# A fused attention and MLP kernel on one core: ScalarE's own SiLU from chunk 1 on, chunk 0 in two token parts, Strassen's scheme in all four groups of chunks 3 to 8, and a new order

## The chip, the cores and the metric

The kernel runs on one core of a Trainium2 chip. The metric is the time of one execution on the device, in microseconds. The runs of the kernel before spread from 271.2 to 278.7 us over the chips of this study, most of them near 273.5 or near 276, so every kernel was timed beside the kernel before on the same chip. A run more than 1.5% above the fastest of its kernel counts as slow and is left out of the ratios. Stages are compared in the profiles, where single instructions have times. Each profile is one execution. All stage times count from the start of the profiled span. The engines are named PE (TensorE, matmuls), DVE (VectorE), ACT (ScalarE), POOL (GpSimd) and SP (SyncE, which here only starts DMAs).

## The reference, cut to what matters

```python
q_s = softmax(q, axis=-1)            # q, k, v: (8, 8, 576, 64) float32
k_s = softmax(k, axis=2)             # over the 576 positions
kv  = einsum('bhsd,bhse->bhde', k_s, v)
x   = einsum('bhsd,bhde->bhse', q_s, kv)   # then (4608, 512)
h   = x @ w_in                       # 512 -> 2048
g   = h * sigmoid(h)                 # SiLU
out = g @ w_out                      # 2048 -> 512, float32
```

## The kernel before

Tokens go through the two layers in nine chunks: chunk 0 has 576 tokens, chunk 1 has 448, the others 512. While chunk t is multiplied, the attention of batch t+1 is prepared. For a batch that means: load q, k and v by DMA; exponentials on ACT (`eq`, `ek`); the sums over q's rows on DVE (`zq`, `rzq`); the normalization of q on POOL (`eq<-eq,rzq`); one transposing DMA of all of q (`qT<-eq`); a cast of v (`vaug`); the kv products on PE, their normalization (`kvn`); and at last the product `o<-qT,kvn`, whose cast is `XT`, the input of the next chunk's first layer. Chunk 2 needs batch 2, so all of this has to be done for batch 2 by the end of chunk 1.

The first layer of chunks 3 to 8 is done in four groups of features, three of them by Strassen's scheme (seven products instead of eight, on sums of weights `TX` and sums of inputs `XS`), the second layer of chunks 1 to 8 wholly by it (sums of weights `TW`, sums of activations `SW`). The sums are made by DVE or POOL. Chunks 0 and 1 compute SiLU by way of tanh (ACT) and a product (DVE), the later chunks by ACT's own SiLU:

```python
STD = 2
def act1(t, fb):
    for off, size in part[t]:
        hps = HP.pop((t, fb, off))
        if t < STD:
            sg = mp.tile([128, TCH], FP32, name="sg", bufs=2)
            nc.scalar.activation(out=sg[:, 0:size], in_=hps[:, 0:size], func=ACT.Tanh, scale=0.5)
        ...
            if t < STD:
                nc.vector.scalar_tensor_tensor(out=y, in0=sg[:, h], scalar=1.0,
                    in1=hps[:, h], op0=ALU.add, op1=ALU.mult)
            else:
                nc.scalar.activation(out=y, in_=hps[:, h], func=ACT.Silu)
```

Each engine is given its instructions in a fixed order, and a table says at which position of a chunk each operation is put. One entry, for chunk 1 (`ex`: exponentials of q and k, `qs`: sums, `qn`: normalization, `vs`: casts of v, `tp`: transposing DMA, all of batch 2):

```python
1: {'ex': [0.9, 4.4, 5.9, 5.4], 'qs': [3.9, 4.9], 'qn': [4.91, 5.91], 'vs': [9.3, 10.9],
    ..., 'tp': 11.4, ...},
...
put(b - 1, p["qs"][cc], qsum, b, cc)
put(b - 1, p["qn"][cc], qnorm, b, cc, G)       # G is GpSimd
```

The prologue handles all of batch 0's q at once and keeps PE busy with dummy matmuls (`heat`) between its steps:

```python
heat(24)
for cc in range(2):
    exp(0, "qt", "eq", cc); qsum(0, cc); qnorm(0, cc, nc.vector)
exp(0, "kt", "ek", 0); vcast(0, 0, nc.scalar)
exp(0, "kt", "ek", 1); vcast(0, 1, nc.scalar)
tr(0, 0); trcopy(0, 0)
heat(5)
kv(0, 0); kvcopy(0, 0)
heat(1)
...
```

The softmax here doesn't subtract the row's maximum and nothing guards it: scores larger than these inputs give would overflow.

Of the kernel before, what the change touches and what calls it, by code (L numbers as in the profile page):

```python
# [15 lines left out]
PLAN = {  # L16
    0: {'y': [5.5, 6.5, 7.5, 8.5, 8.5, 9.5, 10.5, 11.5, 13.5, 13.8, 14.5, 15.5, 15.6, 15.7, 15.9, 22.5], 'ex': [8.9, 10.9, 12.9, 13.4], 'qs': [9.92, 11.4], 'qn': [10.43, 11.41], 'vs': [14.45, 15.05], 'ks': [15.65, 15.75], 'kc': [15.651, 15.751], 'lq': 14.06, 'tp': 12.9, 'ox': [16.35, 16.6], 'oc': [16.36, 18.61], 've': [2, 2]},
    1: {'ex': [0.9, 4.4, 5.9, 5.4], 'qs': [3.9, 4.9], 'qn': [4.91, 5.91], 'vs': [9.3, 10.9], 'ks': [12.4, 13.9], 'kc': [13.41, 14.91], 'lq': 10.45, 'lk': 12.4, 'lv': 15.41, 'tp': 11.4, 'ox': [16.4, 23.6], 'oc': [17.91, 23.61], 've': [1, 1], 'pa': [13.1, 17.7, 18.3], 'pae': [1, 0, 0]},
    2: {'std': 2, 'order': [(3, 1), (2, 1), (2, 6), (3, 6), (2, 2), (2, 7), (3, 2), (3, 7), (3, 5), (2, 5), (2, 4), (3, 3), (3, 4), (2, 3)], 'y': [-2.5, 1.5, 3.5, 4.5, 5.5, 7.5, 9.5, 11.5, 14.0, 15.5, 17.5, 19.0, 20.0, 21.0], 'ex': [-2.6, 0.41, 2.92, 0.43], 'qs': [2.9, 3.9], 'qn': [5.91, 5.91], 'vs': [3.42, 12.4], 'ks': [8.9, 16.4], 'kc': [10.91, 16.41], 'lq': -0.55, 'lk': -2.1, 'lv': 14.41, 'tp': 7.4, 'ox': [18.4, 19.4], 'oc': [18.91, 19.41], 'sl': [0.5, 1.5, 3, 3, 4.5, 8.5, 7, 7], 'add': {(3, 2): 17.02, (2, 7): 13.55, (3, 1): 10.02, (3, 6): 11.55, (2, 5): 17.55, (2, 3): 21.55, (3, 3): 19.55}, 'act': {(2, 6): 13.02, (2, 4): 19.02, (2, 3): 25.02, (2, 5): 17.55, (3, 2): 14.55, (3, 3): 23.02, (2, 1): 11.55, (3, 1): 9.55, (2, 7): 16.02}, 's1': {2: 0, 3: 0}, 'xs': [0.4, 0.9, 7.9, 4.4], 'pa': [16.45, 23.95, 19.45], 'ya': {3: 22.45, 6: 5.5, 5: 15.95, 2: 7.95}, 'm1': [1, 0], 'pb': [-0.4, 0.2, 2.1, 2.2, 2.8], 'xe': [0, 1, 1, 1], 'pae': [1, 1, 1], 'pbe': [0, 0, 0, 0, 0], 've': [1, 2]},
}  # L20
STEADY = {'std': 1, 'order': [(1, 1), (1, 6), (1, 2), (1, 7), (1, 5), (2, 1), (2, 6), (1, 4), (1, 3), (2, 2), (2, 7), (2, 5), (3, 1), (2, 4), (3, 6), (2, 3), (3, 7), (3, 2), (3, 5), (3, 4), (3, 3)], 'y': [1.5, 3.5, 5.5, 7.5, 9.5, 10.0, 15.5, 16.5, 17.5, 18.0, 22.0, 23.5, 24.2, 24.6], 'ex': [-5.1, -0.59, -4.08, -4.57], 'qs': [5.4, 6.4], 'qn': [5.91, 6.41], 'vs': [0.4, 7.42], 'ks': [11.9, 17.4], 'kc': [15.91, 17.41], 'lq': 9.95, 'lk': 16.9, 'lv': 9.41, 'tp': 8.9, 'ox': [22.4, 22.4], 'oc': [22.91, 23.41], 'sl': [2.0, 2.0, 6.5, 4.0], 'add': {(2, 2): 17.02, (1, 2): 6.55, (3, 2): 20.55, (3, 1): 16.55, (3, 7): 21.02, (1, 5): 9.55, (3, 5): 22.55}, 'act': {(1, 5): 12.02, (2, 6): 12.02, (1, 2): 7.02, (3, 1): 19.02, (1, 6): 9.02, (1, 1): 8.02, (3, 3): 25.55, (3, 5): 25.02, (1, 3): 14.02, (2, 2): 15.02, (2, 5): 16.55, (1, 4): 13.02, (3, 7): 23.02, (3, 6): 20.02}, 's1': {1: 1, 2: 0, 3: 0}, 'xs': [-1.6, 0.9, -1.6, 1.4], 'pa': [21.45, 21.95, 23.45], 'pb': [-0.05, 2.46, 2.95, -0.04, 2.95], 'ya': {4: 23.95, 5: 19.45}, 'm1': [0, 0], 'xe': [0, 0, 0, 0], 'pae': [1, 0, 0], 'pbe': [0, 0, 0, 0, 1], 've': [1, 1]}
for _t in range(3, 8):
    PLAN[_t] = STEADY
PLAN[8] = {'std': 1, 'order': [(1, 1), (1, 6), (1, 7), (1, 2), (1, 5), (2, 1), (2, 6), (1, 4), (1, 3), (2, 7), (3, 1), (2, 5), (2, 2), (3, 6), (2, 4), (2, 3), (3, 7), (3, 2), (3, 5), (3, 4), (3, 3)], 'y': [4.5, 5.0, 5.0, 7.5, 9.5, 10.5, 15.5, 17.5, 18.0, 19.0, 22.0, 23.7, 25.5, 26.6], 'sl': [4.0, 10.0, 7.5, 6.0], 'add': {(1, 2): 9.02, (3, 1): 16.02, (1, 5): 9.55}, 'act': {(2, 5): 18.02, (1, 3): 13.02, (1, 4): 15.02, (1, 6): 8.02, (2, 3): 22.02, (3, 3): 25.55, (3, 2): 24.02, (2, 1): 11.02, (3, 5): 22.55, (1, 5): 9.55, (3, 1): 15.55, (1, 2): 8.02, (1, 1): 5.02, (1, 7): 10.02, (2, 4): 19.02, (2, 2): 20.02, (2, 7): 16.02}, 's1': {1: 1, 2: 1, 3: 0}, 'xs': [-11.1, -0.1, 3.4, 7.9], 'pa': [19.95, 20.95, 22.95], 'pb': [-5.55, -4.04, 4.45, -0.04, 2.95], 'ya': {6: 9.5, 3: 27.05, 2: 10.95, 5: 20.95, 1: 7.0, 7: 18.95, 4: 25.7}, 'm1': [0, 0], 'xe': [0, 0, 0, 0], 'pae': [0, 0, 0], 'pbe': [0, 0, 0, 1, 0]}
PLAN[9] = {'y': [0, 1, 2, 3, 4, 5, 6, 7, 8, 9, 10, 11, 12, 13], 'ya': {}, 'm1': [0, 0], 'pb': [-0.5, -0.4, -0.3, 1.9, 2.9], 'pbe': [0, 0, 0, 0, 0]}
TXAT = [(0, (0, 11.76, 1, 0)), (1, (0, 15.77, 1, 0)), (2, (0, 14.78, 1, 1)), (3, (0, 15.79, 1, 1)), (0, (2, 3.1, 0, 0)), (1, (2, 5.6, 0, 0)), (2, (2, 5.6, 0, 0)), (3, (2, 9.6, 0, 1))]
TWAT = [(0, 10.1, 1), (0, 8.7, 1), (0, 13.0, 1), (0, 13.6, 1), (0, 14.7, 0), (0, 19.3, 1), (0, 17.9, 1), (0, 14.0, 1)]

@with_exitstack
def kernel(  # L30
# [26 lines left out]
    part = [[(0, 5 * P), (5 * P, S - 5 * P)]] + [[(0, cut[t + 1] - cut[t])] for t in range(1, NCH)]  # L57
# [34 lines left out]
    def load(b, name, src, ccs=None, eng=nc.sync):  # L92
        if name not in st[b]:
            st[b][name] = ld.tile([128, NG, J * D], FP32, name=name, bufs=LDB[name])
        x = src[b].rearrange("(g r) (p j) d -> g (r p) (j d)", r=2, j=J).rearrange("g x y -> x g y")
        c = slice(0, NG) if ccs is None else slice(2 * ccs, 2 * ccs + 2)
        eng.dma_start(out=st[b][name][:, c, :], in_=x[:, c, :])
# [4 lines left out]
    def exp(b, src, dst, cc):  # L102
        if dst not in st[b]:
            st[b][dst] = ap.tile([128, J, NG * D], BF16, name=dst, bufs=1)
        o = st[b][dst][:, :, cc * 128:(cc + 1) * 128].rearrange("p j (g d) -> p j g d", d=D)
        nc.scalar.activation(out=o, in_=jgd(st[b][src], cc), func=ACT.Exp)  # L106

    def vcast(b, cc, eng):
        o = vaug.rearrange("p j (g e) -> p j g e", e=E1)[:, :, 2 * cc:2 * cc + 2, 0:D]
        if eng is nc.scalar:  # L110
            eng.copy(out=o, in_=jgd(st[b]["vt"], cc))
        else:
            eng.tensor_copy(o, jgd(st[b]["vt"], cc))

    def qsum(b, cc):
# [3 lines left out]
        e = st[b]["eq"][:, :, cc * 128:(cc + 1) * 128].rearrange("p j (g d) -> p j g d", d=D)  # L119
        nc.vector.reduce_sum(out=st[b]["zq"][:, cc], in_=e, axis=AX.X)  # L120
# [15 lines left out]
    def tr_dma(b, eng):  # L136
# [3 lines left out]
        )  # L140

    TG = 6

    def tr(b, g):
        t = ps.tile([128, TG, 128], BF16, name="qtps", tag="ring", bufs=PSB["ring"])
        st[b]["qtps", g] = t
# [541 lines left out]
```

## Time and profile before

The time before the prediction was a median of 272.63 us (272.16 to 273.13, three runs). The profiled execution has a span of 270.6 us. By stages:

| stage | kernel before | length |
|---|---|---|
| first first-layer matmul | 16.65 us | 16.65 |
| chunk 1 starts | 48.90 | 32.25 |
| chunk 2's first 512-column matmul | 69.34 | 20.44 |
| last 128 matmuls start | 251.70 | 182.36 |
| last matmul ends, span ends | 265.79, 270.6 | 4.8 |

From the page of the kernel before: the span, the busy time of the engines with their share, and the busy tenths of PE and the TensorE clock that was granted, in 40 equal slices.

```profile
span 270.6 us, 6388 instructions
PE 255.8 (95%) x2580; PEld 191.9 (71%) x2594; DVE 209.8 (78%) x405; ACT 172.6 (64%) x276; POOL 110.8 (41%) x71
...
PE   8779989987999999999999999999999999999992
...
PEclk9999999997999999999999999999999999999998
```

PE is the limit almost everywhere. It has holes in the prologue and around slices 7 to 10, which is chunk 1. The timeline of PE of the kernel before shows them: start, length, what ran, how often, and in brackets how long PE was idle before it and for what.

```profile
16.65 6.05 PE L233 MATMUL hps<-XT,W 128*128 128x320 bf16 x48
...
48.90 8.96 PE L233 MATMUL hps<-XT,W 128*128 128x448 bf16 x44
58.43 1.67 PE L233 MATMUL hps<-XT,W 128*128 128x448 bf16 x8 [0.57 <-DVE GT L259]
62.01 0.48 PE L168 MATMUL kvps<-vaug,ek 64*64 64x65 bf16 x36 [1.91 <-POOL vaug L113]
...
67.95 0.58 PE L203 MATMUL o<-qT,kvn 64*64 64x384 bf16 x12 [0.84 <-DMA qT<-eq]
...
69.34 2.34 PE L233 MATMUL hps<-XT,W 128*128 128x512 bf16 x7
```

```profile
52.49 2.12 POOL L387 TENSOR_TENSOR TW<-W 128x1024 bf16<-128x1024 bf16 x1
54.58 2.12 POOL L387 TENSOR_TENSOR TW<-W,TW 128x1024 bf16<-128x1024 bf16 x1
56.67 4.18 POOL L126 TENSOR_TENSOR eq<-eq,rzq 128x1152 bf16<-128x1152 bf16 x2
60.81 2.24 POOL L113 CAST vaug<-vt 128x1152 bf16<-128x1152 f32 x2
```

```profile
60.88 3.50 SPq L137 DMA_TRANSPOSE qT<-eq  x1
```

POOL normalizes q from 56.67 to 60.85, the transposing DMA starts at 60.88, and its result is there at 67.95, 7.1 us later.

In the steady chunks PE has no holes. From the windows view of the kernel before, one steady chunk: length, then the busy time of PE, PE's weight loads, DVE, ACT and POOL, each with its count, then clock, DMA share and GB/s.

```profile
178.26:204.81 26.55, 26.50 (x301) 21.54 (x301) 22.91 (x44) 19.21 (x30) 9.84 (x5) 1.00 0.36 78
```

### The profile page before, as it was taken

The numbers are of one execution on the slowest core, as the hardware profiler recorded it, in microseconds if no ns is written. First come the engines' busy times: TensorE is split into PE (matmuls) and PEld (weight loads), VectorE is DVE, ScalarE is ACT, GpSimd is POOL, SyncE is SP. The second block draws the span as 40 slices with busy tenths as digits, with TensorE's granted clock in tenths as the row PEclk, the third lists the DMA queues.
The fourth block names the chain that finished last, engine by engine and source line by source line (L and its number), as shares of the span: only waits on it lengthen the run. The fifth ranks groups of instructions, "written<-read, shape, count | busy, mean of one in ns | idle before, by whom it ended". The sixth has DMA issues, their size and how long they took to land.

```text
span 270.6 us, 6388 instructions
## 1 busy us (share of the span) xinstructions
PE 255.8 (95%) x2580; PEld 191.9 (71%) x2594; DVE 209.8 (78%) x405; ACT 172.6 (64%) x276; POOL 110.8 (41%) x71
## 2 busy tenths in 40 slices
PE   8779989987999999999999999999999999999992
PEld 3456655433568768886888688868886887788882
DVE  2967486596799889887988898879887668877932
ACT  5666576893897598658964995598564447343400
POOL 1552668996287926342624262426223023000000
PEclk9999999997999999999999999999999999999998
DMA  7999999989829740698079607960713012201324
GB/s 255 295 195 245 331 305 207 388 270 241 326 57 368 210 137 1 114 354 306 2 161 385 225 0 148 374 231 18 128 41 79 2 39 63 56 17 25 94 63 116
DMA packets 42925, 46.48 MB, mean 172 GB/s; under 512 B 18576, under 2 KB 30864, under 8 KB 42896
## 3 DMA queue, kind: packets, MB, share of 16 engines
q1 hardware_dynamic: 37856, 38.35, 48.0%
q0 software_dynamic: 5040, 7.73, 12.9%
q8 instruction: 20, 0.33, 0.5%
q14 instruction: 9, 0.07, 0.1%
HBM read 36.70 MB, written 9.44 MB: 171 GB/s over the span
## 4 chain that ended last, share of the span: by engine, by line
PE 61%; DMA 14%; POOL 7%; ACT 6%; issue 5%; SPq 2%; DVE 2%; POOLq 0%; ACTq 0%
PE ops L411 30%; PE hps L316 19%; PE hps L233 8%; DMA W<-in_moe_w_out_dram 8%; DMA kt<-in_k_dram 4%; DMA qT<-eq 3%; POOL eq L126 3%; PE ops L476 2%; POOL TW L387 2%; ACT eq L106 1%; PE kvps L168 1%; ACT ek L106 1%; ACT XT L223 1%; PE o L203 1%; POOL W L516 1%
## 5 line engine op out<-in xcount | busy, mean ns | idle before, releaser
L233 PE MATMUL hps<-XT,W 128*128 128x512 bf16 (+3 forms) x312 | 61.9, 341 | 1.3 <-DVE GT L259 0.6
L411 PEld LDWEIGHTS <-GT 128*128 128x128 bf16 x512 | 50.0, 98 | 8.9 <-issue 0.2
L233 PEld LDWEIGHTS <-W 128*128 128x128 bf16 x320 | 31.4, 99 | 25.0 <-issue 3.5
L411 PEld LDWEIGHTS <-SW 128*128 128x128 bf16 x384 | 37.2, 98 | 5.0 <-DVE SW L371 0.2
L355 ACT ACTIVATE GT<-u 128x512 bf16<-128x512 f32 x40 | 24.5, 629 | 23.6 <-DVE u L333 23.3
L126 POOL TENSOR_TENSOR eq<-eq,rzq 128x1152 bf16<-128x1152 bf16 x14 | 29.9, 2153 | 14.3 <-ACT GT L263 6.7
L316 PE MATMUL hps<-XS,TX 128*128 128x256 bf16 x240 | 35.0, 273 | 0.3 <-ACT GT L263 0.3
L316 PEld LDWEIGHTS <-TX 128*128 128x128 bf16 x320 | 30.7, 98 | 5.3 <-issue 1.8
L259 DVE SCALAR_TENSOR_TENSOR GT<-sg,hps 128x320 bf16<-128x320 f32 (+3 forms) x64 | 23.6, 414 | 12.9 <-ACT sg L247 12.3
L411 PE MATMUL ops<-TW,SW 128*128 128x256 bf16 x256 | 33.0, 273 | 0.0
L411 PE MATMUL ops<-W,GT 128*128 128x256 bf16 x256 | 32.9, 273 | 0.0
L411 PE MATMUL ops<-TW,GT 128*128 128x256 bf16 x256 | 32.9, 273 | 0.0
L333 DVE SCALAR_TENSOR_TENSOR u<-hps,s 128x512 f32<-128x512 f32 x40 | 27.2, 681 | 6.7 <-PE hps L316 5.3
L333 DVE SCALAR_TENSOR_TENSOR u<-hps,u 128x512 f32<-128x512 f32 x40 | 27.4, 686 | 4.0 <-PE hps L316 3.3
L375 POOL TENSOR_TENSOR SW<-GT,SW 128x1024 bf16<-128x1024 bf16 x6 | 13.9, 2320 | 39.1 <-DVE SW L371 27.6
L369 POOL TENSOR_TENSOR SW<-GT 128x1024 bf16<-128x1024 bf16 x7 | 14.9, 2126 | 36.1 <-PE ops L411 36.1
L247 ACT ACTIVATE sg<-hps 128x320 f32<-128x320 f32 (+2 forms) x48 | 21.3, 454 | 11.8 <-PE hps L233 6.3
L316 PEld LDWEIGHTS <-W 128*128 128x128 bf16 x240 | 23.0, 98 | 3.3 <-issue 0.2
L120 DVE TENSOR_REDUCE zq<-eq 128x18 f32<-128x1152 bf16 x16 | 21.3, 1332 | 3.8 <-ACT eq L106 3.8
L316 PE MATMUL hps<-XT,W 128*128 128x256 bf16 x160 | 24.0, 273 | 0.0
L223 ACT CAST XT<-o 128x512 bf16<-128x512 f32 (+3 forms) x36 | 18.2, 561 | 5.7 <-PE o L203 5.7
L106 ACT ACTIVATE eq<-qt 128x1152 bf16<-128x1152 f32 x16 | 18.4, 1161 | 4.5 <-DMA qt<-in_q_dram 4.4
(77 smaller groups left out, 379.7 us busy)
## 6 DMA issues: line engine op xcount, KB each, us to landing
qt<-in_q_dram SPq DMA_DIRECT2D x6, 1152.0 KB, 8.3
kt<-in_k_dram SPq DMA_DIRECT2D x6, 1152.0 KB, 9.6
vt<-in_v_dram SPq DMA_DIRECT2D x6, 1152.0 KB, 6.6
W<-in_moe_w_in_dram POOLq DMA_DIRECT2D x4, 512.0 KB, 10.2
W<-in_moe_w_out_dram POOLq DMA_DIRECT2D x4, 512.0 KB, 17.6
out_dram<-u SPq DMA_DIRECT2D x16, 128.0 KB, 2.4
out_dram<-u SPq DMA_DIRECT2D x32, 64.0 KB, 2.1
qt<-in_q_dram SPq DMA_DIRECT2D x2, 576.0 KB, 4.1
```

Of the source, the lines that this page charges most:

```text
L106: nc.scalar.activation(out=o, in_=jgd(st[b][src], cc), func=ACT.Exp)
L120: nc.vector.reduce_sum(out=st[b]["zq"][:, cc], in_=e, axis=AX.X)
L126: eng.tensor_tensor(out=e, in0=e, in1=r[:, :, :, None].to_broadcast([128, J, 2, D]), op=ALU.mult)
L223: nc.scalar.copy(out=x, in_=o1[g][:, 0:size])
L233: nc.tensor.matmul(out=hps[:, 0:size], lhsT=W1[:, c, fb * 128:(fb + 1) * 128], rhs=XT[t][:, c, off:off + size], start=(c == 0), stop=(c == ...
L247: nc.scalar.activation(out=sg[:, 0:size], in_=hps[:, 0:size], func=ACT.Tanh, scale=0.5)
L259: nc.vector.scalar_tensor_tensor(out=y, in0=sg[:, h], scalar=1.0, in1=hps[:, h], op0=ALU.add, op1=ALU.mult)
L316: nc.tensor.matmul(out=o[:, f, :], lhsT=l(c, 2 * g + f), rhs=r(c), start=bool(first and f == 0 and c == 0), stop=(c == HK - 1), skip_group ...
L333: nc.vector.scalar_tensor_tensor(out=out, in0=o, scalar=1.0, in1=x, op0=ALU.mult, op1=ALU.add)
L355: nc.scalar.activation(out=y, in_=MP[t, g, x], func=ACT.Silu)
L369: V.tensor_add(S1[:, f], quad(t, 0, f, 1), quad(t, 1, f, 1))
L411: nc.tensor.matmul(out=o[:, a, :], lhsT=l(f), rhs=r(f), start=bool(first and a == 0 and f == 0), stop=(f == HF - 1), skip_group_check=True,)
```

## The change

The intent was to spend fewer PE columns (Strassen for the fourth group too), to take tanh's product off DVE in chunk 1, to start chunk 0 earlier by handling only 320 of its 576 tokens in the prologue, and to shorten the end. The core of the diff:

```diff
-    STD = 2
+STD = 1                                  # SiLU on ACT from chunk 1 on
-STEADY = {'std': 1, 'order': [(1, 1), (1, 6), ...
+STEADY = {'std': 0, 'order': [(0, 1), (0, 6), ...   # no direct group left in chunks 3 to 8
-    0: {...}, 1: {'ex': [0.9, 4.4, 5.9, 5.4], 'qs': [3.9, 4.9], 'qn': [4.91, 5.91], ...
+    0: {... 'order': [(0, 0), (4, 0), (1, 0), ...], 'r': [-20.0, -15.0], 'rt': [-4.0, 2.5], 'rx': [3.0, 3.5]},
+    1: {'ex': [-0.204, 3.9, 3.9, 4.4], 'qs': [1.4, 3.9], 'qn': [4.41, 7.41], ...
+WORDER = ['w12', 'x', 'w10', 'w11', 'w13', 'w20', 'w14', 'q', 'w21', 'w15', 'k', 'w22', 'v', 'w23']
     heat(24)
     for cc in range(2):
-        exp(0, "qt", "eq", cc)
-        qsum(0, cc)
-        qnorm(0, cc, nc.vector)
+        exp(0, "qt", "eq", cc, J0)       # J0: the first 320 tokens
+        qsum(0, cc, J0)
+        qnorm(0, cc, nc.vector, J0)
+        tr(0, cc, J0)
     exp(0, "kt", "ek", 0)
-    vcast(0, 0, nc.scalar)
-    ... heat(5) ... heat(1) ... heat(2) ...
+    vcast(0, 0, nc.scalar, (0, 1))
+    vcast(0, 0, nc.vector, (1, 2))
+    ...
+    def rest(cc):                        # the other 256 tokens, put into chunk 0
+        exp(0, "qt", "eq", cc, J1)
+        qsum(0, cc, J1)
+        qnorm(0, cc, nc.vector, J1)
...
+    def halve(eng):                      # tanh leaves out a factor 0.5: 64 tokens of GT[1]
+        x = GT[1][:, :, 0:S - TCH]
+        eng.tensor_scalar_mul(out=x, in0=x, scalar1=0.5)
...                                      # last product split; its stores on two queues
```

`WORDER` is the order in which POOL's queue loads the pieces of the weights (`w10` to `w15`, `w20` to `w23`), the rest of batch 0's q (`x`) and batch 1 (`q`, `k`, `v`). The positions of nearly all operations were set anew as well, and several sums moved from DVE to POOL.

## The prediction

> **What bounds the kernel now.** TensorE. The busy table gives PE 255.8 us of a 270.6 us span. In the timeline eight 128x256 matmuls take 0.87 us, so the layers' columns alone need about 227 us. Read by stage:
> - Prologue: first first-layer matmul at 16.65 us.
> - Chunk 0: 16.65 to 48.9 us, about 31 us of matmul work, 1.3 lost. It is DMA-bound too: the DMA share is about full until the last w_out piece lands at 44.2 us.
> - Chunk 1: 48.9 to 68.5 us for about 13.6 us of matmul work: 6 us lost. The waits name DVE's tanh product (0.57 us) and POOL's late cast of v (1.91 us); then the clock falls (windows view: 0.65 in 62 to 66 us), and eight 448-column matmuls take 2.97 us, not 1.67. The Trainium skill ("TensorE: Matmul & The Clock Gate", Part 1) says an idle PE falls to half clock; this trace agrees.
> - Chunks 3 to 7: 26.55 us each, PE idle under 0.1 us. DVE 22.9, ACT 19.5, POOL 10.5.
> - Tail: 4.8 us after the last matmul.
>
> **What changes.**
> 1. Strassen for a fourth group in chunks 3 to 8: 16 matmuls of 512 columns (8192) become 28 of 256 (7168). 1024 columns x 0.423 ns = 0.43 us per chunk, all on the critical path, 2.6 us in all. DVE gets five adds (0.69 us) and a copy more, but loses 3 XS sums and 4 presums to POOL: it stays near 22 us. POOL rises to about 23 of 26 us (presums 2.1 to 2.4 us each). It should fit, barely.
> 2. SiLU in chunk 1: 16 DVE products (0.6 us) go; tanh (0.54) becomes SiLU (about 0.55). But SiLU and exp need table loads, 1.28 us each here, three in chunk 1 (none with tanh). The Trainium skill ("ScalarE: Activation LUTs", "What ACT_TABLE_LOAD costs") adds a drain of 1.38 us; the trace shows no such gap (load at 73.57, next activation at 74.87). ACT then needs 16 x 0.44 + 4 x 1.05 + 3.9 + copies 1.9 = 17 us, above PE's 13.6: ACT takes over as the limit there. I expect 3 of the 6 us back.
> 3. Prologue: 0.52 MB of q leaves the front (0.59 MB takes about 1.5 us here), v's casts (1.16) are halved over two engines. But first-layer weights still need the same 4.6 MB landed, and the second part's transposes stand before the first-layer matmuls. Chunk 0 stays DMA-bound: about 1 us gained.
> 4. Tail: last product split, two store queues: about 0.5 us.
>
> Sum: 2.6 + 3 + 1 + 0.5 = 7.1, and about 0.7 for the new order: **264.8 us**, 8 times in 10 between **261.5 and 268.5**. Faster by over 2%: 0.77; within 2%: 0.21; slower: 0.02.
>
> **What would show it.** Steady chunks at 26.1 us with PE still gapless (step 1); chunk 1 at about 16.5 us, ACT its busiest engine with three table loads, DVE no longer named in PE's waits (2); chunk 0 ending near 48 us with the last w_out piece still near 44 (3); 4.3 us after the last matmul (4).
>
> **What would make it wrong.** POOL late with presums, so PE waits in every steady chunk (to 268 or more); ACT held in chunk 1 by batch 2's q, and PE at half clock after it; PE at half clock when chunk 0 starts. The other way, chunk 1 and the prologue without stalls: 260.

## The result, and the profile after

The kernel with the change is slower: a median of 281.50 us (281.18 to 281.67, six runs) against 273.57 us (272.16 to 275.39, six runs) for the kernel before. The ratio is 1.0284, with a 95% interval of 1.0239 to 1.0328. Ratios here are the mean time of one kernel's fast runs over that of the other's of the same rounds, so they are not quite the ratios of the medians quoted.

| stage | before | after | difference |
|---|---|---|---|
| first first-layer matmul | 16.65 us | 18.18 us | +1.5 |
| chunk 1 starts | 48.90 | 55.51 | +6.6 in all |
| chunk 2's first 512-column matmul | 69.34 | 78.56 | chunk 1: 20.44 to 23.05, +2.6 |
| last 128 matmuls start | 251.70 | 260.39 | from there: 182.36 to 181.83, -0.5 |
| span | 270.6 | 279.4 | end: 4.8 to 4.9 |

The four differences (6.6 + 2.6 - 0.5 + 0.1) make the 8.8 us between the spans. None of the four has the predicted size, and the two largest, in chunks 0 and 1, have the other sign. The page of the kernel after:

```profile
span 279.4 us, 6587 instructions
PE 257.0 (92%) x2651; PEld 199.5 (71%) x2658; DVE 210.0 (75%) x388; ACT 181.7 (65%) x293; POOL 178.4 (64%) x111
...
PEclk9858999997999999999999999999999999999999
```

PE is not less busy although it has fewer columns to do. Part of its work ran at a lower clock, as the PEclk line shows; but also in a steady chunk, at a clock of 1.00, its busy time fell only from 26.50 to 26.44 us (below). POOL's busy time rose by 68 us. The timeline of PE of the kernel after, at the same places as before:

```profile
18.18 1.25 PE L245 MATMUL hps<-XT,W 128*128 128x320 bf16 x4 [3.33 <-DMA W<-in_moe_w_in_dram]
19.41 0.61 PE L156 MATMUL qtps<-ident,eq 128*128 128x128 bf16 x4
...
23.95 3.98 PE L245 MATMUL hps<-XT,W 128*128 128x320 bf16 x32
...
55.51 0.55 PE L245 MATMUL hps<-XT,W 128*128 128x448 bf16 x2
...
66.79 4.87 PE L245 MATMUL hps<-XT,W 128*128 128x448 bf16 x16 [2.53 <-ACT GT L275]
...
77.17 0.57 PE L214 MATMUL o<-qT,kvn 64*64 64x384 bf16 x12 [1.38 <-DMA qT<-eq]
```

In the kernel before, 48 first-layer matmuls ran in 6.05 us from 16.65. Here four matmuls take 1.25 us (half speed), and the unbroken stream begins only at 23.95, because the transposes and the attention product of the other 256 tokens stand between the first matmuls on PE. From 18.18 to 23.95 PE shows hardly a wait (busy 5.52 of 5.77 us): at half clock it is as slow as the chain through ACT and DVE that feeds it. That this chain alone would hold it as long, the run a_heat shows. Windows view, the stretch from 16 to 24 us, first the kernel before, then the kernel after:

```profile
16.00:24.00 8.00, 7.65 (x62) 5.65 (x59) 6.38 (x22) 5.62 (x14) 2.58 (x4) 1.00 1.21 199
```

```profile
16.00:24.00 8.00, 5.57 (x33) 3.22 (x34) 5.40 (x12) 3.25 (x8) 4.49 (x6) 0.59 1.31 195
```

The clock of 0.59 is what an idle PE gets afterwards; the Trainium skill ("TensorE: Matmul & The Clock Gate", Part 1) says that an idle window drops the clock to one half, and this trace agrees (single stretches of it read 0.50).

Chunk 1 ends, as before, with the transposing DMA. The timelines of POOL and of SP's queue of the kernel after show the same chain:

```profile
62.59 2.38 POOL L138 TENSOR_TENSOR eq<-eq,rzq 128x1152 bf16<-128x1152 bf16 x1 [2.24 <-issue]
64.93 2.56 POOL L311 TENSOR_TENSOR TX<-W 128x1024 bf16<-128x1024 bf16 x1
67.44 1.16 POOL L122 CAST vaug<-vt 128x1152 bf16<-128x1152 f32 x1
68.56 2.11 POOL L138 TENSOR_TENSOR eq<-eq,rzq 128x1152 bf16<-128x1152 bf16 x1
```

```profile
70.70 2.75 SPq L148 DMA_TRANSPOSE qT<-eq  x1
```

A sum of weights and a cast of v stand between the two halves of the normalization, so the transposing DMA starts at 70.70 instead of 60.88. Counted from the start of the chunk that is 15.2 us instead of 12.0, so 3.2 us later. One of the reasons for the lateness is on ACT, whose timeline in the kernel after has the second exponential of q behind four SiLUs and a table load, and the next SiLU behind another:

```profile
60.32 1.28 ACT L113 ACT_TABLE_LOAD   x1
61.62 1.16 ACT L113 ACTIVATE eq<-qt 128x1152 bf16<-128x1152 f32 x1
62.69 2.20 ACT L113 ACTIVATE ek<-kt 128x1152 bf16<-128x1152 f32 x2
64.90 1.28 ACT L275 ACT_TABLE_LOAD   x1
66.20 2.73 ACT L275 ACTIVATE GT<-hps 128x448 bf16<-128x448 f32 x6
```

The steady chunks did not become shorter. A steady chunk of the kernel after in the windows view:

```profile
162.56:189.22 26.66, 26.44 (x313) 22.62 (x313) 23.13 (x41) 21.59 (x34) 21.31 (x12) 1.00 0.67 198
```

PE is idle for 0.22 us of it, where it was idle for 0.05 before, and the period is 0.1 us longer instead of 0.43 us shorter. The idle time is not the whole loss: around it, four matmuls begin at 161.74 and the next four at 162.56, 0.82 us apart, where other fours stand 0.44 us apart. How much hangs on this wait the run a_pre will show. The timelines of DVE and POOL of the kernel after, just before PE's wait at 162.56 ("0.22 <-DVE SW L396"):

```profile
160.37 1.34 DVE L394 TENSOR_TENSOR SW<-GT 128x1024 bf16<-128x1024 bf16 x1
161.81 0.69 DVE L396 TENSOR_TENSOR SW<-SW,GT 128x1024 bf16<-128x1024 bf16 x1
```

```profile
159.02 2.14 POOL L400 TENSOR_TENSOR SW<-GT,SW 128x1024 bf16<-128x1024 bf16 x1
```

In the kernel before, POOL is quiet beside the same DVE sum:

```profile
177.84 0.69 DVE L369 TENSOR_TENSOR SW<-GT 128x1024 bf16<-128x1024 bf16 x1
```

In the kernel after, POOL works until 161.16, and the sum takes 1.34 us instead of 0.69. The Trainium skill ("GPSIMD Engine Reference", Specifications) says that GpSimd shares its interfaces to SBUF with VectorE and that VectorE instructions with two inputs in SBUF contend with it; the trace agrees.

The end did not get shorter: in SP's queue of the kernel after, the last stores still stand behind each other.

```profile
273.85 1.26 SPq L510 DMA_DIRECT2D out_dram<-s  x2
275.21 1.19 SPq L499 DMA_DIRECT2D out_dram<-u  x2
```

The last matmul ends at 274.48. Splitting the product halved DVE's last operation from 0.69 to 0.42 us, so the result is there at 274.93. But SP is busy with the two stores before until 275.11, and the last ones start at 275.21. The wait for the queue eats the 0.27 us; this was all that the split could give, in place of the 0.5 us that were forecast.

### The profile page after: what moved, and what is told of

It is laid out like the page before. It is cut to its first block, busy times and chain, and to the rows that moved or that the text cites. A ratio compares the mean times of both kernels' runs of the same rounds, so it can differ in the third digit from the quotient of the medians.

```text
span 279.4 us, 6587 instructions
## 1 busy us (share of the span) xinstructions
PE 257.0 (92%) x2651; PEld 199.5 (71%) x2658; DVE 210.0 (75%) x388; ACT 181.7 (65%) x293; POOL 178.4 (64%) x111
## 4 chain that ended last, share of the span: by engine, by line
PE 71%; DVE 11%; DMA 5%; POOL 4%; ACT 1%; issue 1%; DVEq 0%; ACTq 0%; POOLq 0%
PE ops L439 31%; PE hps L338 26%; PE hps L245 7%; PE ops L524 4%; DMA W<-in_moe_w_in_dram 3%; DMA qT<-eq 2%; DVE SW L394 2%; DVE zq L130 2%; PE kvps L172 2%; DVE u L356 2%; PE o L214 1%; DVE TX L311 1%; DVE SW L396 1%; DVE GT L271 1%; POOL TX L311 1%
## 5 line engine op out<-in xcount | busy, mean ns | idle before, releaser
L245 PE MATMUL hps<-XT,W 128*128 128x320 bf16 (+3 forms) x222 | 41.9, 337 | 8.1 <-DMA W<-in_moe_w_in_dram 3.3
L356 DVE SCALAR_TENSOR_TENSOR u<-hps,s 128x512 f32<-128x512 f32 x52 | 35.5, 683 | 14.8 <-PE hps L338 14.8
L338 PE MATMUL hps<-XS,TX 128*128 128x256 bf16 x312 | 44.7, 273 | 1.1 <-POOL XS L295 1.1
L338 PEld LDWEIGHTS <-TX 128*128 128x128 bf16 x416 | 40.2, 98 | 7.7 <-issue 2.6
L380 ACT ACTIVATE GT<-u 128x512 bf16<-128x512 f32 x52 | 32.5, 628 | 19.5 <-DVE u L356 18.8
L398 POOL TENSOR_TENSOR GT<-GT 128x1024 bf16<-128x1024 bf16 x13 | 27.7, 2129 | 0.1
L130 DVE TENSOR_REDUCE zq<-eq 128x18 f32<-128x1152 bf16 (+2 forms) x18 | 21.8, 1210 | 5.3 <-ACT eq L113 5.3
L380 ACT ACTIVATE GT<-s 128x512 bf16<-128x512 f32 x26 | 16.3, 627 | 11.1 <-DVE s L356 11.0
L271 DVE SCALAR_TENSOR_TENSOR GT<-sg,hps 128x320 bf16<-128x320 f32 (+2 forms) x48 | 14.9, 349 | 9.7 <-ACT sg L259 9.1
L396 POOL TENSOR_TENSOR SW<-SW,GT 128x1024 bf16<-128x1024 bf16 x9 | 19.6, 2177 | 2.4 <-DVE SW L394 1.9
```

The costliest lines, as they stand in the source:

```text
L130: nc.vector.reduce_sum(out=st[b]["zq"][:, cc, js], in_=e, axis=AX.X)
L245: nc.tensor.matmul(out=hps[:, 0:size], lhsT=W1[:, c, fb * 128:(fb + 1) * 128], rhs=XT[t][:, c, off:off + size], start=(c == 0), stop=(c == ...
L338: nc.tensor.matmul(out=o[:, f, :], lhsT=l(c, 2 * g + f), rhs=r(c), start=bool(first and f == 0 and c == 0), stop=(c == HK - 1), skip_group ...
L356: nc.vector.scalar_tensor_tensor(out=out, in0=o, scalar=1.0, in1=x, op0=ALU.mult, op1=ALU.add)
L380: nc.scalar.activation(out=y, in_=MP[t, g, x], func=ACT.Silu)
L396: V.tensor_sub(S2[:, f], S1[:, f], quad(t, 0, f, 0))
```

## The experiments

Eighteen kernels ran; all gave correct results. Stage times of the profiled runs (us), with the ratio to the kernel before:

| run | first matmul | chunk 1 | chunk 2 | chunk 2 to last 128 | span | ratio, 95% interval |
|---|---|---|---|---|---|---|
| before | 16.65 | 48.90 | 69.34 | 182.36 | 270.6 | 1 |
| after | 18.18 | 55.51 | 78.56 | 181.83 | 279.4 | 1.0284 (1.0239-1.0328) |
| a_tanh1 | 18.26 | 55.73 | 80.10 | 181.63 | 280.7 | 1.0279 (1.0217-1.0342) |
| a_q2 | 17.30 | 54.20 | 73.50 | 181.75 | 274.2 | 1.0094 (1.0028-1.0160) |
| a_w10 | 14.47 | 58.08 | 81.35 | 181.79 | 282.1 | 1.0341 (1.0289-1.0392) |
| a_heat | 18.81 | 56.01 | 76.97 | 182.04 | 278.0 | 1.0173 (1.0118-1.0228) |
| after_ref | 18.15 | 55.36 | 78.31 | 181.79 | 279.0 | 1.0297 (1.0204-1.0389) |
| a_pre | 18.12 | 54.83 | 77.80 | 179.67 | 276.4 | 1.0214 (1.0119-1.0310) |
| a_x | 15.52 | 54.24 | 77.72 | 181.77 | 278.3 | 1.0219 (1.0122-1.0315) |
| a_xk | 15.48 | 53.84 | 76.64 | 181.79 | 277.2 | 1.0228 (1.0113-1.0343) |
| a_one | 17.16 | 53.43 | 76.25 | 181.81 | 276.9 | 1.0208 (1.0130-1.0285) |
| best1 | 17.22 | 53.73 | 73.88 | 179.68 | 272.4 | 1.0074 (1.0004-1.0143) |
| a_c0 | 16.22 | 49.08 | 73.91 | 181.77 | 274.5 | 1.0131 (1.0049-1.0213) |
| best2 | 16.42 | 49.79 | 72.37 | 180.89 | 272.0 | 0.9962 (0.9902-1.0022) |
| b_silu | 15.85 | 48.40 | 70.24 | 180.16 | 269.2 | 0.9915 (0.9847-0.9982) |
| best3 | 16.01 | 49.38 | 71.91 | 179.68 | 270.4 | 0.9889 (0.9831-0.9947) |
| before_q | 16.79 | 48.97 | 72.83 | 182.34 | 274.0 | 1.0085 (1.0004-1.0166) |
| best4 | 16.39 | 49.57 | 69.33 | 184.82 | 273.1 | 1.0128 (1.0066-1.0191) |
| best5 | 17.08 | 50.65 | 73.69 | 184.17 | 276.8 | 1.0104 (1.0046-1.0162) |
| best6 | 15.59 | 48.20 | 71.16 | 179.65 | 269.6 | 0.9929 (0.9857-1.0001) |

"Chunk 1" and "chunk 2" are the starts of their first layers. The last 128 matmuls are taken from the chain of work of each profile, which shows starts 0.16 us later than the timeline does, in every run alike. after and after_ref are the same kernel and differ by up to 0.25 us, but the start of chunk 1 of kernels with the same chunk 0 (a_c0, best2, b_silu, best3, best6) spreads over 1.6 us, so smaller differences there show nothing by themselves. The end of chunk 1 carries one more chance: the transposing DMA of batch 2's q took 4.6 to 10.0 us from issue to landing (7.0 in before, 6.4 in after, 4.6 in a_q2, 10.0 in best1). Each row is one execution, not always a typical one: a_q2's is the fastest of its four runs, best2's and best5's are the slowest of their six. Ratios hang on the spread of the kernel before as well.

### a_tanh1: tanh again in chunk 1

```diff
-STD = 1
+STD = 2
```

> The changed kernel with one constant changed: chunk 1 goes through tanh and a DVE product again, so there are no table loads in chunk 1. In the changed kernel chunk 1 takes from 55.5 us (its first matmul) to 77.7 us (matmuls steady again after batch 2's XT products), 22.2 us, against 19.6 before. Theory S (ScalarE's three table loads of 1.28 us and the exps between them set chunk 1's length): it shortens by 3 us or more, and the kernel takes about 278.5 us. Rival Q (chunk 1 ends when batch 2's q has been through exp, sum, POOL's normalization and the transposing DMA; POOL has a TX sum and a cast of v between the two normalizations, and those stay): under 1 us either way, 281 us, and the transposing DMA is still issued near 70.7 us.

The median was 282.48 us, and chunk 1 became longer, not shorter: PE waited for DVE's product five times, 2.45 us at most. Going back to tanh while everything else stays gains nothing. That does not clear the table loads, since DVE's product took their place as the thing that PE waits for in an order made for SiLU. The chain of batch 2's q came at about the same time (transposing DMA at 69.61).

### a_q2: batch 2's q early in chunk 1

```diff
-1: {'ex': [-0.204, 3.9, 3.9, 4.4], 'qs': [1.4, 3.9], 'qn': [4.41, 7.41],
+1: {'ex': [-0.204, -0.203, -0.202, -0.201], 'qs': [0.2, 0.3], 'qn': [3.45, 3.46],
```

> The changed kernel with only chunk 1's order changed: all four exps of batch 2 stand together in front of the SiLUs (one table load in place of three), DVE sums q before its TX sums, POOL normalizes both parts of q one after the other, before its TX sum. SiLU stays. Theory Q: the transposing DMA is issued near 64.5 us, not 70.7, matmuls are steady again from about 72 us, not 77.7, and the kernel takes about 276 us. Theory S alone (two table loads saved, the q chain free): about 2.6 us less, 279 us.

The median was 277.90 us (275.96 to 278.71). The transposing DMA started at 63.12 instead of 70.70, and chunk 1 (first matmul to chunk 2's) took 19.3 us instead of 23.05. This is the largest effect of an edit within one chunk. It has two parts that the run does not separate: PE's wait for the transposing DMA (1.38 us) is gone, and, since the exponentials now stand together and two of three table loads are saved, its wait for SiLU fell from 2.53 to 0.42 us. What PE waits for then is in its timeline in a_q2:

```profile
68.80 0.83 PE L172 MATMUL kvps<-vaug,ek 64*64 64x65 bf16 x72 [2.23 <-POOL vaug L122]
```

POOL's cast of v, which stands behind the normalization and a sum of weights, takes over. The chain is not gone, only shorter.

### a_w10: the weights of the first blocks loaded first

```diff
-WORDER = ['w12', 'x', 'w10', 'w11', ...
+WORDER = ['w10', 'w12', 'x', 'w11', ...
-'r': [-20.0, -15.0], 'rt': [-4.0, 2.5], 'rx': [3.0, 3.5]
+'r': [3.2, 3.3], 'rt': [4.5, 5.5], 'rx': [5.6, 5.7]      # and one block moved in the order
```

> The changed kernel with the first weight pieces loaded in the order in which TensorE uses them (the first 256 columns of w_in first, the rest of q third), and the second token part of q handled after the first matmuls, not before. Theory W (TensorE waits 3.3 us for the third piece in the queue, and its clock is halved by that wait): first first-layer matmuls at 15 to 15.5 us, not 18.2, chunk 1 starts 3 to 4 us earlier than 55.5 us, the kernel takes about 278 us. Rival D (chunk 0 is bound by all that the DMA has to bring, whose last piece lands at 45.7 us): matmuls start earlier but chunk 1 starts within 1 us of 55.5 us, about 281 us.

The first matmul came at 14.47 us, and the kernel became slower (284.44 us). PE then waited 2.19 us for the other 256 tokens' normalization at 22.64, and the clock was 0.50 in the windows 14 to 18 and 24 to 30 us. Chunk 1 began at 58.08, 2.6 us later than in after, which neither theory had expected. Here the early start was worth nothing, since the rest of the attention stood in the stream a few microseconds later.

### a_heat: dummy matmuls in the prologue again

```diff
+    heat(3)     # and 2, 3, 2, 12 more at the later steps of the prologue
```

> The changed kernel with 22 idle matmuls on a zero tile put into the prologue's gaps (the kernel before had such matmuls there), nothing else. The first first-layer matmul stays near 18.2 us, since it waits for its weights. Theory H (from 18.2 to 23 us TensorE ran at a granted clock of 0.50 because it had been idle): the clock is 1.00 there, chunk 0 gets 2 to 2.4 us shorter, and the kernel takes about 279.3 us. Rival D (chunk 0 bound by the DMA): under 0.5 us.

The clock was 1.00 in all windows, and chunk 1 began at 56.01, no earlier: the stream still began only at 23.86, since PE waited for DVE, for q's normalization (0.42 us) and for a copy of `qT` (0.94 us). So the half clock at the start of chunk 0, one of the dangers that the prediction named, was really there but hidden behind the chain of the other 256 tokens. From its first matmul to chunk 1, PE was busy for 33.3 of 37.2 us here, and for 34.9 of 37.3 us in after: what the clock gave back became waiting.

The median was 279.54 us, 2 us less than after's, and chunk 2 came 1.6 us earlier. The traces name the place: the transposing DMA was issued at 70.68, as in after (70.70), but landed after 4.6 us and not after 6.4, and PE did not wait for it:

```profile
75.52 0.63 PE L214 MATMUL o<-qT,kvn 64*64 64x128 bf16 x16
```

Nothing in chunk 1 was edited, so this is the clearest sign that the landing of batch 2's q sets the end of chunk 1 in the changed kernel. Why it landed sooner no run shows.

### after_ref, a_pre, a_x, a_xk: one chip, four kernels

after_ref is the changed kernel itself, run again as the measure for the three others.

> The changed kernel as it is, to stand beside the next three on the same chip: 281.5 us, within 1%. Chunk 1 starts near 55.5 us, chunk 2 near 77.7 us, steady chunks last 26.65 us.

It gave 281.69 us, as expected.

A presum is one of the sums `SW` of activations. a_pre gives POOL's three presums of a steady chunk new places, so that POOL is quiet while DVE does its own two:

```diff
-'pb': [1.45, 1.46, 5.95, 1.46, 1.95]
+'pb': [1.45, 1.46, 1.95, 1.97, 1.94]
```

> The changed kernel with the order of three of POOL's sums at each steady chunk's start changed, nothing else: the first one is put behind the DVE sums SW that TensorE waits for, so that POOL is quiet while DVE does them. In the changed kernel the DVE sum takes 1.34 us there (0.69 in the kernel before, where POOL was quiet) and TensorE waits 0.4 us for it in every chunk. Theory C (DVE slowed by POOL's sums, which use up the fourth group's 0.43 us): the sum takes 0.69 us, a steady chunk 26.15 to 26.25 us in place of 26.65, the kernel takes 2 to 2.5 us less. Rival N (TensorE loses its time in the new order of products itself): still 26.6 us or more.

The time was 279.60 us (278.18 to 280.06) against after_ref's 281.69 (280.83 to 282.25), and the steady chunks took 26.20 us. From chunk 2 to the last 128 matmuls it is 179.67 us, 2.1 less than in after_ref and 2.7 less than in the kernel before. DVE's sum in a_pre:

```profile
132.57 0.68 DVE L394 TENSOR_TENSOR SW<-GT 128x1024 bf16<-128x1024 bf16 x1
```

It is back from 1.34 to 0.68 us, and PE is busy for all of a steady chunk. So the first term of the prediction was right in mechanism, and lost by two engines meeting. Its size was right in part by luck: a steady chunk became 0.35 us shorter (26.55 to 26.20), not 0.43, which over six chunks makes 2.1 us; the rest of the 2.7 lies outside them, as does the 0.5 us that after gained although its steady chunks were longer.

a_x loads the other 256 tokens' q by SyncE behind v, ahead of the weights; a_xk also puts the exponentials of batch 1's k later:

```diff
-WORDER = ['w12', 'x', 'w10', 'w11', ...      'rt': [-4.0, 2.5]
+WORDER = ['x', 'w10', 'w12', 'w11', ...      'rt': [1.5, 2.5]
-'ex': [14.3, 14.3, 24.8, 20.3]
+'ex': [14.3, 14.3, 27.0, 27.2]               # a_xk only
```

> The changed kernel with the rest of q loaded by SyncE right behind v, not by POOL between the weights, the first weight piece then in front, and the rest's transposes behind the first two matmuls. Theory R (chunk 0 starts late because the second token part's attention work stands in TensorE's order in front of the first layer and waits for its q, which lands at 17 us): full-rate matmuls from about 20 us, not 23.9, and chunk 1 starts 3 to 4 us earlier, 52 us. Rival K (chunk 0 waits later for batch 1's k, which lands at 38 us and for which ScalarE stands still with tanh behind it): matmuls start earlier, wait longer at 36 to 42 us, and chunk 1 starts within 1.5 us of 55.5 us.

> As the run before, and the two exps of batch 1's k stand 3 and 7 places later in ScalarE's order, just before its casts of v. Theory R alone: no more than the run before, or 1 us worse since they come late. Rival K: no wait of ScalarE for k with tanh behind it, TensorE busy through 36 to 42 us, and chunk 1 starts 2 us earlier than in the run before.

Chunk 1 began at 54.24 and 53.84, 1.1 to 1.5 us earlier than in after_ref, of the 6.6 us that were looked for, and within the spread of this stage. The medians were 279.55 and 279.53 us. Neither the late load nor the early exponentials are the cause by themselves.

### a_one and best1: all of batch 0's q in front, the new order kept

a_one undoes the two token parts (all of q in the prologue, dummy matmuls as before, `w10` loaded first, the exponentials of k late) and keeps the halved casts of v and the new order of chunk 0. best1 adds a_q2's edit, with the cast of v right behind the normalization, and a_pre's.

```diff
-    put(0, PLAN[0]["r"][cc], rest, cc)        # and rt, rx
+    pass
-        load(0, "qt", q, cc, js=J0)
+        load(0, "qt", q, cc)
```

> The changed kernel with the two token parts undone: all of q is loaded in front again and goes through exp, sum, normalization and transposes in the prologue, with the kernel before's 8 matmuls on a zero tile between, and the first weight pieces in the order of use; batch 1's k exps late, as in the run before. The halved casts of v stay. Theory P (the second part's chain of DVE work in the middle of chunk 0 and the cold clock cost what the split was to save): first-layer matmuls at full clock from 16.5 to 17 us, chunk 1 starts at 49.5 to 50.5 us, against 55.5 in the changed kernel and 53.8 in the run before, and the kernel takes about 276 us. Rival E (the new order of chunk 0 itself, or the 1.5 us later last weight piece, is at fault): chunk 1 not before 53 us, 279 us.

> The run before, with the two other repairs: batch 2's exps, sums and normalizations together in chunk 1 (and its casts of v right behind them on POOL), and POOL's sum moved away from DVE's at the start of each steady chunk. If the three causes add up, 281.5 - 5.5 - 5 - 2.4 = about 268.5 us, faster than the kernel before by 1.5 to 2.5%. If they hide one another (the slot that one frees is lost at the next wait), 271 us or more.

Chunk 1 began at 53.43 in a_one, only 2.1 us earlier than in after, where 5 to 6 had been expected; the median was 278.82 us. In its prologue the kv product waited 2.42 us for DVE's half of the cast of v (DVE was at q), and in chunk 0 PE waited for DVE's products (0.52, 1.22 and 0.50 us) and for two weight pieces (0.39 and 0.35 us). So undoing the two token parts, together with the early `w10` and the late exponentials, gave a third of the loss in chunk 0, as long as the rest of the change was in place. a_xk, which kept the two parts, came almost as far (53.84). best1 took 274.99 us, not the 268.5 of a plain sum. The steady chunks' edit gave its 2.1 us again; chunk 1's gave 2.7 (22.82 to 20.15), where a_q2's gave 3.7, and its transposing DMA, with 10.0 us, made PE wait for 1.18. Chunk 0 is still the largest loss.

### a_c0 and best2: chunk 0 as in the kernel before

a_c0 takes the prologue, the weight order, the casts and the whole order of chunk 0 from the kernel before; the rest is as in after. best2 adds the chunk 1 and steady edits of best1.

```diff
-    0: {'y': [11.0, 15.5, 17.0, ...], ..., 'order': [(0, 0), (4, 0), (1, 0), ...
+    0: {'y': [11.5, 13.5, 15.5, ...], ..., 'order': [(0, 0), (0, 1), (1, 0), ...
-WORDER = ['w12', 'x', 'w10', 'w11', 'w13', 'w20', ...
+WORDER = ['w16', 'w17', 'w20', 'w14', 'w21', 'q', ...    # w16, w17: w_in's first two quarters
```

> The changed kernel with the prologue and all of chunk 0 as they are in the kernel before: no token parts in the attention work, the casts of v whole on ScalarE, the weight pieces and their order, and the order of chunk 0's operations; chunk 1 and everything after it as in the changed kernel. Theory O (all of chunk 0's loss lies in this stage: its prologue and, for more than half, its new order of operations, since the run with only the parts undone still started chunk 1 at 53.4 us): chunk 1 starts at 48.5 to 49.5 us, chunk 2 about 21 to 22 us later, and the kernel takes about 275.5 us. Rival M (chunk 0 is held by what the changed kernel does for later chunks, above all POOL's and DVE's sums of weights): chunk 1 not before 51.5 us.

> The run before with the two other repairs (batch 2's q, k and v work together in chunk 1, POOL's sum away from DVE's in the steady chunks). If the repairs add: chunk 1 starts at 49 us, chunk 2 at 68 to 69 us, steady chunks of 26.2 us, and the kernel takes about 269 us, 1 to 1.5% less than the kernel before. If chunk 1 gets no shorter than its 19 to 20 us, as in the last run: about 271 us.

In the timeline of PE of a_c0, chunk 1 begins at the old place:

```profile
49.08 5.24 PE L245 MATMUL hps<-XT,W 128*128 128x448 bf16 x24
...
62.61 6.12 PE L245 MATMUL hps<-XT,W 128*128 128x448 bf16 x16 [4.56 <-ACT GT L275]
```

The whole new chunk 0, prologue included, thus cost 6.4 of the 6.6 us, give or take the 1.6 us by which this start spreads. Of these, a_one's edit gave 2.1, and going on to the old casts, weight order and placement gave the other 4.3. Which of these last three weighs most is not separated; the waits in a_one (2.42 us for the halved cast, 2.2 us for DVE's products, 0.7 us for weights) suggest that all three take part, but no run tests it.

But only 4.65 of the 6.4 us arrive at chunk 2 (73.91 against 78.56), chunk 1 having taken 24.8 us where 21 to 22 were expected, and in best2 even less: it begins chunk 1 3.9 us earlier than best1 and chunk 2 only 1.5 us earlier. best2's PE and ACT timelines say why:

```profile
58.82 8.92 PE L245 MATMUL hps<-XT,W 128*128 128x448 bf16 x32 [3.79 <-ACT GT L275]
```

```profile
54.70 2.22 ACT L113 ACTIVATE ek<-kt 128x1152 bf16<-128x1152 f32 x2 [1.75 <-DMA kt<-in_k_dram]
56.94 1.28 ACT L275 ACT_TABLE_LOAD   x1
```

Batch 2's k lands at 54.70. ACT, which has its exponentials in front of the SiLUs, stands idle for it, and the SiLUs start at 58.23, while PE's six result banks are full. Chunk 0's gain runs into a load that did not come earlier by as much (it lands at 56.65 in best1). best2 took 272.16 us (ratio 0.9962): no difference from the kernel before is shown. Its profile is of its slowest run (273.91 us).

With the cause of chunk 1 still open, six more kernels ran.

### b_silu, best3 and before_q: what bounds chunk 1

b_silu puts the first six SiLUs of chunk 1 in front of the exponentials of k. best3 also takes POOL out of chunk 1's chain: the normalization, the `halve` and three weight sums go to DVE. before_q is the kernel before with q's exponentials, sums and normalization at the front, the normalization on DVE.

```diff
-'ex': [-0.204, -0.203, -0.202, -0.201]        # best2
+'ex': [-0.204, -0.203, 5.2, 5.3]              # b_silu, best3
-'qn': [3.45, 3.46], 'tp': 8.9                 # best2, b_silu
+'qn': [0.25, 0.35], 'tp': 0.36                # best3, and V instead of G for batch 2
```

```diff
-1: {'ex': [0.9, 4.4, 5.9, 5.4], 'qs': [3.9, 4.9], 'qn': [4.91, 5.91], ... 'tp': 11.4   # before
+1: {'ex': [0.9, 0.95, 5.9, 5.4], 'qs': [0.96, 0.97], 'qn': [0.965, 0.975], ... 'tp': 0.98
```

> best2 with one change: in chunk 1 the two exponentials of batch 2's k stand behind the first six SiLUs on ScalarE instead of in front of them (one more pair of table loads, 2.57 us). In best2 ScalarE sat idle 1.75 us for the DMA of k, then did the exponentials (2.2 us) and the table load (1.28 us), while six finished first-layer blocks waited, and TensorE waited 3.79 us for them; chunk 2 began at 72.37. Theory T (ScalarE's order of exponentials, table load and SiLU is what makes chunk 1 long once batch 2's q is early): the wait of 3.79 us falls below 1 us, no TensorE wait above 1.5 us takes its place, chunk 2 begins by 70.0, the span falls by over 2 us. Rival P (GpSimd's chain: TW sums to 59.5, normalization of q to 64.6, cast of v to 67.3, sets the end of chunk 1): the 3.79 us shrink but TensorE then waits for GpSimd's cast of v instead, and chunk 2 begins at 71.5 to 72.5 all the same.

> b_silu with GpSimd taken out of chunk 1's chain: the normalization of batch 2's q, the half of GT and three of the TW and TX sums go from GpSimd to VectorE (where a sum takes 0.63 to 0.69 us when GpSimd is quiet, 2.45 to 2.60 when it is busy), and the transposing DMA is queued right after. Rival P: chunk 2 begins at 66 to 68.5, the TX and TW sums on VectorE take about 0.7 us, TensorE waits under 1.5 us in all in chunk 1; the time is 267 to 269.5, under the kernel before by more than 1%. Theory T alone: no better than b_silu within 0.7 us.

> The kernel before with only batch 2's q chain made early: both exponentials of q at the front of chunk 1, its normalization on VectorE instead of GpSimd, the transposing DMA queued right after. If batch 2's q chain sets the end of chunk 1 in the kernel before as well (theory Q): chunk 2's first 512-column matmul comes at 66.0 to 68.0 instead of 69.34, the waits for the transposing DMA (0.84 us) and for GpSimd's cast of v (1.91 us) go, the time falls by 1.5 to 3 us (ratio 0.990 to 0.995). If VectorE's tanh products set it, the 1.4 us added to VectorE make chunk 1 longer: 69.5 to 71.

b_silu: 272.12 us, ratio 0.9915. Chunk 2 began 2.1 us earlier than in best2, of which 1.4 us are the earlier start of chunk 1, so that chunk 1 itself is 0.7 us shorter. The wait of 3.79 us is gone, but another one, of 2.87 us, stands behind the second pair of table loads, and 0.91 us go to POOL's cast of v. Neither theory holds as it was written.

best3: 271.76 us (270.04 to 272.84), ratio 0.9889, the lowest ratio; its interval lies below 1. The gain of 1.1% is against runs of the kernel before from 272.73 to 276.67 us on that chip; on other chips that kernel's fastest runs (271.2 to 271.8) are as fast as best3. Its chunk 2 did not come at 66 to 68.5 as rival P expected, but at 71.91: batch 2's q landed late (ACT waited 1.88 us for it), and PE waited 1.81 and 2.87 us for SiLU. So POOL's chain is not what bounds chunk 1 here. What the run does show is the contention. The same sum of weights on DVE, in best2 with POOL busy beside it and in best3 with POOL quiet:

```profile
60.05 2.60 DVE L412 TENSOR_TENSOR TW<-W 128x1024 bf16<-128x1024 bf16 x1
```

```profile
62.60 0.68 DVE L412 TENSOR_TENSOR TW<-W 128x1024 bf16<-128x1024 bf16 x1
```

A sum that POOL does in 2.1 us can thus cost DVE 1.9 us on a sum that runs at the same time, where DVE would have done the moved sum itself in 0.7 us: more is lost than won. The Trainium skill ("Perfetto Trace Analysis", Optimizing Scalar/DVE Operations) warns that moving work between these two might not help; the trace gives the size.

before_q was not faster than the kernel before (276.24 us, ratio 1.0085, interval 1.0004 to 1.0166). Chunk 2 came at 72.83. With DVE busy with q from 52.02 to 59.0, its tanh products came late:

```profile
59.66 6.04 PE L233 MATMUL hps<-XT,W 128*128 128x448 bf16 x24 [4.76 <-DVE GT L259]
```

Theory Q expected 66.0 to 68.0, its rival 69.5 to 71. The run shows that an early q bought with DVE's time does not pay in the kernel before, as DVE's products are then what PE waits for. What an early q would give that costs DVE nothing, it does not show.

### best4 and best5: only the steady chunks of the change

best4 is the kernel before in chunks 0 to 2, with chunks 3 to 8 of a_pre. best5 also puts two `TW` sums on POOL behind the cast of v.

```diff
-STD = 1
+STD = 2                    # PLAN[1], PLAN[2], TXAT and TWAT as in the kernel before
-TWAT = [..., (0, 31.69, 1), (0, 31.62, 1), ...]   # best4
+TWAT = [..., (1, 11.1, 1), (1, 11.0, 1), ...]     # best5 only
```

> The kernel before in chunks 0 to 2 (tanh in chunk 1, its orders and engines), with the change's chunks 3 to 8 (Strassen in all four groups) and the presum moved out of the way as in a_pre. Of the change only its first term is left. If that term stands by itself (theory C with the chip's contention removed): chunk 2's first 512-column matmul near 69.4 as in the kernel before, steady chunks 26.15 to 26.25 us, the last 128 matmuls begin 179.6 to 180.5 us after chunk 2's start (182.4 in the kernel before), span 267.5 to 268.5, time 269 to 271, ratio 0.985 to 0.993. If the term needs the change's chunks 1 and 2 around it, TensorE waits at the seam (chunk 3's start) by over 1 us and the gain is under 1.5 us.

> best4 with one change in chunk 1: the two TW sums that GpSimd does before the normalization of batch 2's q come after the cast of v. Theory Q (GpSimd's queue before the normalization sets the end of chunk 1): the normalization ends at about 59.8 instead of 60.9 and the cast at about 62, the transposing DMA is queued by 59.9 and chunk 2 begins 0.8 to 1.2 us earlier than in best4. If VectorE's tanh products or ScalarE's exponentials set it: chunk 2 begins within 0.4 us of best4.

best4 took 276.13 us (ratio 1.0128). Chunk 2 began where it does in the kernel before (69.33), the steady chunks took 26.21 us, and most of the gain was lost at one seam, in the timeline of PE of best4:

```profile
103.26 1.04 PE L439 MATMUL ops<-TW,SW 128*128 128x256 bf16 x4 [2.64 <-DVE SW L396]
```

The first steady chunk waits for a presum, and the matmuls after it run at the lower clock for a while (1.06 us for four instead of 0.60). The orders of neighbouring chunks belong together: here the steady chunks could not be set behind another kernel's chunk 2 without a new order. best5 was not better (275.73 us, 274.78 to 278.70). Its profile is of its slowest run: POOL was done with q at 62.2, no earlier than in best4 (61.5), because the whole of chunk 1 began 1.1 us later, and PE then waited 4.01 us for the transposing DMA, which took 8.8 us here and 6.4 in best4. Theory Q's expectation (0.8 to 1.2 us earlier) was not met; with such a profile and such a spread of times it is not refuted either.

### best6: k's exponentials behind the tenth SiLU

```diff
-'ex': [-0.204, -0.203, 5.2, 5.3]     # best3
+'ex': [-0.204, -0.203, 9.6, 9.7]     # and the SiLUs 7 to 10 in front of them
```

> best3 with the two exponentials of batch 2's k behind the tenth SiLU of chunk 1 instead of the sixth. TensorE can run six blocks (six PSUM banks, 0.74 us each) ahead of ScalarE; a SiLU takes 0.45 us, so after six of them three finished blocks still wait, and the 4.77 us of table load, exponentials and table load stop TensorE 2.87 us; after ten of them hardly any wait. Theory T2 (it is where the pair of table loads stands): the wait of 2.87 us falls below 0.8 us, chunk 2 begins at 69.0 to 70.3 instead of 71.91, time 269 to 270.5, ratio 0.979 to 0.986. Rival (ScalarE's total work bounds chunk 1 anyway): the wait only moves, to the cast of v, the kv products or the last SiLUs, and chunk 2 begins within 0.7 us of best3.

The wait for SiLU fell from 4.7 us in all to 1.0, but chunk 2 began 0.75 us earlier only (71.16), with chunk 1 begun 1.2 us earlier, and the median was 271.56 us, no different from best3 (ratio 0.9929). PE's timeline in best6:

```profile
61.92 0.48 PE L172 MATMUL kvps<-vaug,ek 64*64 64x65 bf16 x36 [1.23 <-ACT ek L113]
65.12 0.48 PE L172 MATMUL kvps<-vaug,ek 64*64 64x65 bf16 x36 [2.72 <-DVE kvn L192]
```

The wait moved to the kv product and its normalization, as the rival said. ACT's work in chunk 1 (casts 1.84 and 1.56, exponentials 4.44, SiLUs 7.4, `kvn` 0.5, three table loads 3.85, from its timeline) is 19.6 us, about as long as the chunk of the kernel before (20.4); and its exponentials cannot start before batch 2 lands. With SiLU, chunk 1 was shorter than 20.4 us only behind a late chunk 0, and by little (a_q2 19.3 us, best1 20.2 us).

## Why the prediction was wrong

The prediction said 264.8 us and "faster"; the kernel was slower by 2.8%. Its four terms and what the profile and the experiments showed:

1. **"1024 columns x 0.423 ns = 0.43 us per chunk, all on the critical path, 2.6 us in all"**: the mechanism was right, and nothing of it arrived: steady chunks of 26.66 us, 0.1 longer than before, in place of 26.1. The failed step is "It should fit, barely": I added up busy times of POOL and DVE as if each kept its speed beside the other. The list of what could go wrong named POOL being late; it was DVE being slowed by POOL, 1.34 instead of 0.69 us. a_pre got 2.1 us back by new places for POOL's presums, with steady chunks of 26.20 us.

2. **"I expect 3 of the 6 us back"** in chunk 1: it was 2.6 us longer. The failed step is "ACT takes over as the limit there". The sum of ACT's work was about right (17 us forecast; the windows view gives 16.9 us busy from 55.51 to 78.56), but the chunk took 23.05 us: a sum of one engine's work was not what bounded it. Chunk 1 of the changed kernel ends when batch 2's q has gone through load, exponential, sum, POOL, transposing DMA and product. The new order issued that DMA 3.2 us later in the chunk, and in a_heat, where the DMA took 1.8 us less, the chunk was 2.1 us shorter. Before that, PE waited 2.53 us for SiLUs behind table loads and exponentials. a_q2 got 3.7 us back by mending both, and how much of it each gave is not shown. Nor did SiLU pay afterwards: in best2 ACT stood idle for k, and in best6 its work in chunk 1 had grown to 19.6 us.

3. **"Chunk 0 stays DMA-bound: about 1 us gained"**: 6.6 us lost, the largest error. The failed step is "stays DMA-bound": I took the landing of the weights as the limit and so thought of the prologue and the order as free to change. But the last w_out piece landed only 1.5 us later than before (45.7 instead of 44.2), and chunk 1 began 6.6 us later. The kernel after waited 3.33 us for a weight piece that is third in its queue, then went through the transposes and the product of the rest of q, and its stream began 7.3 us later than before. a_c0 showed that the new chunk 0 cost 6.4 us; undoing the two parts with two smaller edits gave 2.1 of it (a_one). The half clock that I had warned of was there and cost chunk 0 nothing that a_heat could give back.

4. **"Tail: last product split, two store queues: about 0.5 us"**: nothing. The split could give 0.27 us (DVE's last operation of 0.42 instead of 0.69 us), and the wait for SP's queue, still busy with the stores before, took that.

The 0.7 us for "the new order" had no ground in the profile at all. The range (261.5 to 268.5) was too narrow as well: of the three dangers named, PE at half clock came in chunk 0 and in chunk 1 (0.50 from 68 to 70 us), the presums came late by way of DVE, and ACT was held in chunk 1, though by table loads and its own order and not by the landing of q. Only the presums had been given a number.

What stays open: which of casts, weight order and placement weighs most in the 4.3 us of chunk 0 beyond a_one's edit; how a_q2's 3.7 us divide between q's chain and the table loads; why the transposing DMA took 4.6 us in one run and 10.0 in another; and the spread of the kernel before.

## What to carry to other kernels

Follow the last wait of each stage back to where its data was loaded before touching the engines in between, because a stage whose end is set by one long chain through several engines gets longer when a link of it is put behind other work, and a gain ahead of it can be swallowed by a load that did not move (best2: 3.9 us earlier at its start, 1.5 at its end). Do not count GpSimd's time as free for two-input sums: a sum moved there can slow one of VectorE's own by more than it saves (1.9 us against 0.7 here), so place the two engines' sums apart in time. Change one stage of a tuned order at a time and time it, since here the presums' places (2.1 us), the order of one chunk's exponentials (3.7 us) and one prologue with its chunk (6.4 us) together weighed more than the whole gain that was forecast (8 us), and the best repaired version (best3, 0.9889 of the time before) finally gained about 1%.

## What the Trainium skill lacked or had wrong

- "ScalarE: Activation LUTs", What ACT_TABLE_LOAD costs: it states about 1283 ns for the load and about 1380 ns of drain. The load is 1.28 us here, but in the kernel after the next activation starts 0.02 us after it (load 64.90 to 66.18, SiLU at 66.20), and the load itself starts 0.01 us after the last exponential ended. No gap of the drain's length stands beside a table load in the traces.
- "GPSIMD Engine Reference", Specifications: this section says that the two engines contend and gives no size (other parts of the skill say more). Sums of 128x1024 in bf16 with both inputs in SBUF took DVE 0.68 us with POOL quiet, 1.34 us when POOL worked for part of the time, and up to 2.60 us with POOL busy throughout; DVE's sums with an input in PSUM kept their 0.69 us beside POOL (at 159.76 in the kernel after).
- "Advanced Engine Details and Errata", X-Bar Transpose (TRN2): it says that transposing DMAs are as fast as regular ones and expects 350 to 400 GB/s. Here 0.59 MB (18 blocks of 128x128 in bf16) took 4.6 to 10.0 us from issue to landing beside other transfers, which is 59 to 128 GB/s (0.59 MB over those times). Regular loads of 0.59 MB in the prologue had medians of 4.1 to 8.7 us in the kernel before. So the two kinds are alike, as the page says, and the expected rate was not reached by a single DMA among others; its rate alone no run shows.
